# Two unused tiles that shift the start of gates, x and weight slots in SBUF

## The chip, the cores and the metric

One core of one Trainium2 chip runs the whole program. The metric is device time in microseconds (us) for one execution, from inputs in HBM to the output in HBM; lower is better. The engines named below are PE (TensorE: matmuls, with its weight loads shown as PEld), DVE (VectorE), ACT (ScalarE), POOL (GpSimd) and SP, whose queue (SPq) issues every DMA.

## The reference

Three layers in a row, with float32 results (the weights arrive as 8-byte floats):

```python
# 1. attention over chunks of 32 positions: q, k, v are (4, 8, 768, 64)
scores = scale * q_c @ k_full.T          # k_full: 8 memory rows + 16 left + 32 + 8 right
a = softmax(scores); out = a @ v_full
# x: (3072, 512), heads side by side
# 2. first gated layer, 512 -> 1536 -> 512
y = (sigmoid(x @ w_gate) * (x @ w_val)) @ w_out
# 3. second gated layer, 512 -> 2048 -> 512
h = y @ w2_in
result = (h * sigmoid(1.702 * h)) @ w2_out
```

## The kernel before, in words

**Tiling.** The 3,072 rows are cut into six blocks of 512 (`BLK`). Attention runs in 32 tiles of 96 rows, six of them ahead of the first block (the prologue), the rest beside the first gated layer. Blocks of x are kept transposed, 128 partitions by four groups (`NK`) of 512 columns. Each gated layer loops over blocks and, inside, over `f`, slices of 128 of the hidden width (`F1` = 12, then `F2` = 16).

**Split numbers.** Every operand of the large matmuls is held as a high part and a low part in a 32-bit format (F32R): `xh` and `xl`, `gh` and `gl` (the gates), and for each weight a slot of 128 x 2 x 512, high in the first 2,048 bytes of a partition and low in the next. A product is three matmuls: high by high, high by low, low by high.

**The matmuls.** All large matmuls have a stationary block of 128 x 128 (512 bytes in each partition) and stream a moving operand of 128 x 512 (2,048 bytes in each partition). `first_product` (lines 719 to 738) has the weight slot as stationary and x as moving: eight matmuls at L726, over four groups of `xh` and `xl` in turn, and four at L733 with the low weights. `gemm2` (L890, matmuls at L897) has `w_out` as stationary and `gh` or `gl` as moving, 12 a slice. `gemm4` (L993) calls `mm3` (L704): there the gate is stationary and the weight slot is moving, 12 a slice. `gated` (L742) makes the gates: a sigmoid (L750), a product (L753), the high copy (L756) and the low rest (L760). It takes the two buffers `sig0/sig1`, `gh0/gh1`, `gl0/gl1` in turn, so consecutive values of `f` use different ones.

**SBUF.** Each pool lays its tiles one behind the other, in the order in which they are opened. The long-lived pool `cp` holds, in this order, the raw and staging tiles, `sig`, `gh`, `gl`, the x tiles, one set of attention buffers (`main`, L771) and the first `NW - NLATE` of the 36 weight slots, ten of them (L779). Behind it the pool `pro` holds the prologue's attention buffers for six tiles. When the prologue has been issued, `open_late` (L810) closes `pro` and opens the other slots over the same bytes, and among them, in places that four slots take later, two raw tiles (`raw_s`), the buffers `qkn_a` and `pw_a` and an identity matrix `ident_a` for the next attention tiles. The framework makes the first use of such bytes wait for the last use of what lay there.

**Order.** `Schedule` (L32) simulates all tasks with assumed costs and due times and issues them in the resulting order; each engine then runs its own instructions in that order. Tile addresses don't enter its costs. The gate of a slot's first write (`gate`, L847 to L863) goes by the number `u` of the conversion, not by the pool in which the slot lies: from `u` = 8 (`NXR`) on, the task is ordered behind `open_late`. The weights are converted by `convert` (L231) in that order.

Of the kernel before, what the change touches and what calls it, by code (L numbers as in the profile page):

```python
# [8 lines left out]
F32 = mybir.dt.float32  # L9
# [9 lines left out]
P = 128  # L19
# [112 lines left out]
def kernel(  # L132
# [42 lines left out]
    cp = ctx.enter_context(tc.tile_pool(name="cp", bufs=1))  # L175
# [7 lines left out]
    def ring(n, shape, dtype, tag):  # L183
        return [cp.tile(shape, dtype, tag=f"{tag}{i}", name=f"{tag}{i}") for i in range(n)]
# [3 lines left out]
    NSR = 30  # L188
    raw = ring(NRAW, [P, 512], I64, "raw")
    fts = ring(NF + NST, [P, 512], F32, "f")  # L190
    sigs = ring(2, [P, BLK], F32, "sig")
    ghs = ring(2, [P, BLK], F32R, "gh")
    gls = ring(2, [P, BLK], F32R, "gl")
# [10 lines left out]


    NW = 3 * F1
    NLATE = 26
    slots = {}

    def new_slots(pool, names):  # L210
        for s in names:
            slots[s] = pool.tile([P, 2, 512], F32R, tag=f"w{s}", name=f"w{s}")
# [557 lines left out]

    main = Bufs(cp, "", ["vn", "qt", "kt", "e", "mx", "sm", "pt"])  # L771
    main.gate = None
    order = []
    for f in range(F1):
        order.append((3 * f, f, cols(w_gate, f)))
# [2 lines left out]
    order.sort(key=lambda u: u[0])  # L778
    new_slots(cp, [u[1] for u in order[: NW - NLATE]])  # L779

# [25 lines left out]
    def spare(i, shape, dtype, name):  # L806

        return late_pool[0].tile(shape, dtype, tag=f"w{order[NW - 1 - i][1]}", name=name)

    def open_late():  # L810
        pro_stack.close()
        late_pool.append(ctx.enter_context(tc.tile_pool(name="cp2", bufs=1)))
        new_slots(late_pool[0], [u[1] for u in order[NW - NLATE : NW - 4]])
        sraw.extend(spare(i, [P, 512], I64, f"raw_s{i}") for i in (3, 2))
# [268 lines left out]
```

## Time and profile before

| | |
|---|---|
| median of two timed runs | 1259.62 us (1259.45 and 1259.78) |
| profiled execution, device time | 1264.35 us |
| its span, first to last instruction | 1262.6 us |
| granted PE clock, mean of the span | 0.989 of full speed |
| PE busy | 1231.8 us (98%) |
| DVE, ACT, POOL busy | 620.2, 475.0, 236.0 us |

A busy time counts an engine as busy while any instruction is in it; neighbouring matmuls overlap in the record, so the rate of matmuls is read from the distance between their starts or from the length of a run of them, not from the length of one. The profiled execution lies 1.75 us outside its span and 4.7 us above the median; differences are worked out inside the profiled execution and then set against the median.

### The profile page before, as it was taken

Reading aid. Unit: us, or ns where it says so; the run is one execution under the profiler, and the core shown is the slowest. Engines: PE = TensorE matmul, PEld = TensorE weight load, DVE = VectorE, ACT = ScalarE, POOL = GpSimd, SP = SyncE. Lnnn points to the kernel's source line nnn. Section 1 sums busy time; section 2 is a strip of 40 time slices with the busy share of each in tenths; the row PEclk is TensorE's granted clock in tenths of the full one; section 3 lists DMA queues with packets and bytes.
Section 4 is the critical chain, followed back from the end, with each engine's and each line's share of the span. In section 5 each row is a group of like instructions: output and inputs, shape, how many; then the busy total and the mean of one; then the engine's idle time right before and its main releaser. Section 6 shows DMA issues by size and latency. Waiting matters only on the chain.

```text
span 1262.6 us, 18066 instructions
## 1 busy us (share of the span) xinstructions
PE 1231.8 (98%) x7120; PEld 987.7 (78%) x7120; DVE 620.2 (49%) x1161; ACT 475.0 (38%) x754; POOL 236.0 (19%) x198
## 2 busy tenths in 40 slices
PE   7799899999999999999999999999999999999998
PEld 5677777777777887787788788888888888888886
DVE  6979852786488528816677711122322222222322
ACT  4687742342244224313576632222222222322212
POOL 2465740010000001000365642110010000100000
PEclk9699999999999999999999999999999999999999
DMA  9556522223022202400365410010100200100000
GB/s 205 147 164 179 136 57 67 41 49 69 18 52 49 63 10 49 94 2 18 118 186 157 132 67 1 17 50 1 50 17 1 67 1 1 67 1 1 34 1 34
DMA packets 166036, 78.03 MB, mean 62 GB/s; under 512 B 132542, under 2 KB 153278, under 8 KB 165950
## 3 DMA queue, kind: packets, MB, share of 16 engines
q1 hardware_dynamic: 165950, 76.87, 23.5%
q8 instruction: 56, 0.92, 0.3%
q14 instruction: 30, 0.25, 0.1%
HBM read 64.24 MB, written 12.58 MB: 61 GB/s over the span
## 4 chain that ended last, share of the span: by engine, by line
PE 90%; DVE 5%; DMA 1%; ACT 1%; issue 1%; POOL 1%; SPq 1%; DVEq 0%; POOLq 0%; ACTq 0%
PE bank L726 33%; PE bank L704 21%; PE bank L733 17%; PE bank L897 14%; PE bank L645 2%; PE bank L495 1%; DVE f L276 1%; DVE pw L563 1%; SPq L305 1%; POOL pw_a L563 1%; PE bank L585 0%; DVE raw_s L262 0%; DVE raw L271 0%; DVE raw L262 0%; DVE sm L552 0%
## 5 line engine op out<-in xcount | busy, mean ns | idle before, releaser
L726 PE MATMUL bank<-xh,w 128*128 128x512 f32 x960 | 382.4, 398 | 2.3 <-ACT w L281 2.0
L726 PE MATMUL bank<-xl,w 128*128 128x512 f32 x960 | 380.9, 397 | 0.0
L753 DVE TENSOR_TENSOR sig<-bank,sig 128x512 f32<-128x512 f32 x168 | 115.9, 690 | 434.1 <-ACT sig L750 337.3
L733 PE MATMUL bank<-xh,w 128*128 128x512 f32 x960 | 264.1, 398 | 0.0
L750 ACT ACTIVATE sig<-bank 128x512 f32<-128x512 f32 x168 | 100.6, 599 | 389.6 <-PE bank L733 389.3
L704 PE MATMUL bank<-w,gh 128*128 128x512 f32 x768 | 241.0, 395 | 0.0
L726 PEld LDWEIGHTS bank<-xh,w 128*128 128x128 f32 x960 | 181.5, 189 | 47.9 <-ACT w L281 2.3
L726 PEld LDWEIGHTS bank<-xl,w 128*128 128x128 f32 x960 | 181.5, 189 | 43.3
L733 PEld LDWEIGHTS bank<-xh,w 128*128 128x128 f32 x960 | 179.3, 188 | 42.8
L756 ACT ACTIVATE gh<-sig 128x512 fp32r<-128x512 f32 x168 | 106.2, 632 | 197.4 <-DVE sig L753 190.3
L704 PEld LDWEIGHTS bank<-w,gh 128*128 128x128 f32 x768 | 144.6, 188 | 33.7
L897 PE MATMUL bank<-gh,w 128*128 128x512 f32 x576 | 159.6, 399 | 0.0
L704 PE MATMUL bank<-w,gl 128*128 128x512 f32 x384 | 151.1, 393 | 0.0
L897 PEld LDWEIGHTS bank<-gh,w 128*128 128x128 f32 x576 | 108.5, 190 | 26.5 <-DVE f L918 0.2
L760 DVE TENSOR_TENSOR gl<-sig,gh 128x512 fp32r<-128x512 f32 x128 | 91.0, 711 | 74.5 <-ACT gh L756 74.2
L285 POOL TENSOR_TENSOR w<-f,w 128x512 fp32r<-128x512 f32 x68 | 96.2, 1428 | 62.7 <-ACT w L281 61.1
L563 POOL TENSOR_TENSOR raw<-e,sm 96x448 f32<-96x448 f32 x21 | 21.6, 1029 | 410.8 <-DVE sm L555 410.8
L704 PEld LDWEIGHTS bank<-w,gl 128*128 128x128 f32 x384 | 72.2, 188 | 17.1
L946 POOL TENSOR_TENSOR xl<-f,xh 128x512 fp32r<-128x512 f32 x24 | 31.4, 1318 | 279.9 <-ACT xh L943 279.9
L897 PE MATMUL bank<-gl,w 128*128 128x512 f32 x288 | 79.7, 398 | 0.0
L620 DVE STREAM_TRANSPOSE pt<-raw 32x256 f32<-32x256 f32 x168 | 73.1, 435 | 2.6
L760 POOL TENSOR_TENSOR gl<-sig,gh 128x512 fp32r<-128x512 f32 x40 | 55.7, 1391 | 73.3 <-ACT gh L756 68.7
(84 smaller groups left out, 908.6 us busy)
## 6 DMA issues: line engine op xcount, KB each, us to landing
raw<-in_moe_w_out_dram SPq DMA_DIRECT2D x24, 512.0 KB
raw<-in_moe_w_in_dram SPq DMA_DIRECT2D x16, 512.0 KB
y_dram<-f SPq DMA_DIRECT2D x24, 256.0 KB
f<-y_dram SPq DMA_DIRECT2D x24, 256.0 KB
out_dram<-f SPq DMA_DIRECT2D x23, 256.0 KB
vn<-in_v_dram SPq DMA_DIRECT2D x24, 240.0 KB
raw<-in_moe_w_gate_dram SPq DMA_DIRECT2D x8, 512.0 KB
raw<-in_moe_w_val_dram SPq DMA_DIRECT2D x8, 512.0 KB
```

Of the source, the lines that this page charges most:

```text
L285: nc.gpsimd.tensor_tensor(out=w[:, 1, :], in0=ft, in1=w[:, 0, :].bitcast(F32), op=ALU.subtract)
L563: eng.tensor_tensor(out=dst, in0=e3()[r, :, c], in1=T["sm"][r].to_broadcast([n, H, keys[1] - keys[0]]), op=ALU.mult)
L620: nc.vector.transpose(T["pt"][r * CH : (r + 1) * CH, :, c * CH : (c + 1) * CH], T["pn"][c * CH : (c + 1) * CH, :, kb * CH : (kb + 1) * CH],)
L704: nc.tensor.matmul(ps_out, a, c, start=(first and i == 0 and j == 0), stop=(last and i == n - 1 and j == 2),)
L726: nc.tensor.matmul(bank[bk][:, :n], w[:, 0, ts[t]], x[xb][:, t, :n], start=t == 0 and x is xhs, stop=False)
L733: nc.tensor.matmul(bank[bk][:, :n], w[:, 1, ts[t]], xhs[xb][:, t, :n], start=False, stop=t == NK - 1)
L750: nc.scalar.activation(sig[:, :n], bank[src_sig][:, :n], AF.Sigmoid, scale=scale)
L753: nc.vector.tensor_tensor(out=sig[:, :n], in0=bank[src_val][:, :n], in1=sig[:, :n], op=ALU.mult)
L756: nc.scalar.activation(gh[:, :n], sig[:, :n], AF.Copy)
L760: eng.tensor_tensor(out=gl[:, :n], in0=sig[:, :n], in1=gh[:, :n].bitcast(F32), op=ALU.subtract)
L897: nc.tensor.matmul(bank[Y[m]][:, :n], w[:, wi, m * P : (m + 1) * P], g[:, :n], start=f == 0 and j == 0, stop=f == F1 - 1 and j == 2,)
L946: nc.gpsimd.tensor_tensor(out=xls[xb][:, m, :], in0=st[:, :BLK], in1=xhs[xb][:, m, :].bitcast(F32), op=ALU.subtract)
```

## The change

Two tiles that nothing writes or reads are opened in `cp`: `pad0`, 224 x 4 = 896 bytes a partition, ahead of `sig0`, and `pad1`, 112 x 4 = 448 bytes, behind `main` and ahead of the weight slots. `NLATE` goes from 26 to 27, so that nine slots lie in `cp` and the tenth is opened by `open_late`, as the first of the late ones. With that, `sig`, `gh`, `gl`, `xh`, `xl` and all slots begin at multiples of 2,048 bytes.

```diff
@@ -188,6 +188,7 @@
     raw = ring(NRAW, [P, 512], I64, "raw")
     fts = ring(NF + NST, [P, 512], F32, "f")
+    cp.tile([P, 224], F32, tag="pad0", name="pad0")
     sigs = ring(2, [P, BLK], F32, "sig")
     ghs = ring(2, [P, BLK], F32R, "gh")
@@ -204,7 +205,7 @@
     NW = 3 * F1
-    NLATE = 26
+    NLATE = 27
     slots = {}
@@ -770,6 +771,7 @@
     main = Bufs(cp, "", ["vn", "qt", "kt", "e", "mx", "sm", "pt"])
     main.gate = None
+    cp.tile([P, 112], F32, tag="pad1", name="pad1")
     order = []
```

## Rows read from the trace of the kernel before

**Rows 1.** Page, part 1: busy us, share of the span, instructions by engine.

```profile
PE 1231.8 (98%) x7120; PEld 987.7 (78%) x7120; DVE 620.2 (49%) x1161; ACT 475.0 (38%) x754; POOL 236.0 (19%) x198
```

**Rows 2.** Busy time by stretches: stretch, length, then each engine's busy us, granted clock.

```profile
core 0: us, PE busy (x) PEld busy (x) DVE busy (x) ACT busy (x) POOL busy (x), PEclk, DMA share, GB/s
...
49.17:54.88 5.71, 5.71 (x14) 4.45 (x14) 5.68 (x6) 3.59 (x6) 4.21 (x3) 0.50 1.13 285
...
75.00:200.00 125.00, 117.23 (x765) 92.67 (x766) 88.74 (x131) 81.97 (x131) 69.17 (x60) 0.97 0.50 131
200.00:734.00 534.00, 533.84 (x3481) 425.99 (x3480) 338.16 (x732) 215.19 (x323) 93.16 (x71) 1.00 0.28 69
734.00:1253.00 519.00, 519.00 (x2234) 419.39 (x2233) 128.32 (x182) 130.25 (x215) 43.65 (x34) 1.00 0.06 21
```

**Rows 3.** Chain that ended last, 725 to 742 us: start us, us, what, how many.

```profile
728.57 3.73 PE bank L726 x16
...
734.18 2.79 PE bank L704 x12
736.97 1.87 PE bank L726 x8
738.84 2.76 PE bank L704 x12
```

**Rows 4.** The same stretches by line: two rows L726, two L733, then L704, L897.

```profile
200.00:734.00 534.00, 238.09 (x945) 177.17 (x944) 1.00 0.28 69
734.00:1262.60 528.60, 186.66 (x736) 138.02 (x736) 1.00 0.07 23
...
200.00:734.00 534.00, 130.10 (x476) 88.53 (x476) 1.00 0.28 69
734.00:1262.60 528.60, 100.92 (x369) 69.04 (x368) 1.00 0.07 23
...
734.00:1262.60 528.60, 282.37 (x1152) 216.61 (x1151) 1.00 0.07 23
...
200.00:734.00 534.00, 195.66 (x716) 133.48 (x715) 1.00 0.28 69
```

**Rows 5.** Who waited, PE from 200 us on: us in total, times, longest.

```profile
PE bank L726 <- ACT sig L750: 0.2, 1, 0.2
```

**Rows 6.** PE in order of time, 736 to 739 us: start us, us, instruction.

```profile
736.81 0.39 PE L726 MATMUL bank<-xh,w 128*128 128x512 f32 x1
...
737.28 0.40 PE L726 MATMUL bank<-xh,w 128*128 128x512 f32 x1
...
737.74 0.40 PE L726 MATMUL bank<-xh,w 128*128 128x512 f32 x1
...
738.21 0.40 PE L726 MATMUL bank<-xh,w 128*128 128x512 f32 x1
...
738.67 0.63 PE L704 MATMUL bank<-w,gh 128*128 128x512 f32 x2
```

**Rows 7.** The same view, 740 to 742 us.

```profile
740.07 0.62 PE L704 MATMUL bank<-w,gh 128*128 128x512 f32 x2
...
741.44 0.86 PE L733 MATMUL bank<-xh,w 128*128 128x512 f32 x3
```

**Rows 8.** The same view, first and last of twelve matmuls at half clock.

```profile
49.76 0.63 PE L726 MATMUL bank<-xl,w 128*128 128x512 f32 x1
...
54.45 0.59 PE L726 MATMUL bank<-xh,w 128*128 128x512 f32 x1
```

**Rows 9.** Chain, 86 us: transposes, each with a weight load of its own.

```profile
86.37 0.44 PE bank L386 x4
```

**Rows 10.** All engines in order of time, 44 to 50 us.

```profile
44.30 2.83 PE L645 MATMUL bank<-pt,vn 128*64 128x96 f32 x32
...
47.29 0.35 SPq L305 DMA_DIRECT2D qkn_a<-in_k_dram  x1
47.34 0.21 POOL masks.py:197 MEMSET ident_a<- 128x128 f32 x1 [5.10 <-PE bank L645]
...
49.17 0.51 SPq L253 DMA_DIRECT2D raw_s<-in_moe_w_gate_dram  x1
```

## The prediction

> **What bounds the kernel now.** I read the engines' busy times first: PE is busy for 98% of the span and no other engine for half of it [rows 1]. Then the stretches: from 200 us to 1,253 us PE has no gap to speak of, at a granted clock of 1.00, while DVE falls to 128 us of the last 519 [rows 2]. The view of waits says the same: from 200 us on PE waited 0.2 us for other engines [rows 5]. Before 200 us PE is not the only bound: 117.2 of 125 us busy between 75 and 200, with the clock not always at full [rows 2]. So after 200 us the time is the number of matmuls times the distance between their starts, and nothing else that the change touches counts there. The number: 945 + 736 at L726, 476 + 369 at L733, 1,152 at L704 and 716 at L897 make 4,394 of the large kind [rows 4]. The distance, from the chain that ended last: 16 matmuls in 3.73 us, or 233.1 ns; 12 of L704 in 2.79 us, or 232.5 ns; the next 12 of L704 in 2.76 us, or 230.0 ns [rows 3]. At 233.1 ns the 4,394 take 1,024 us of the 1,062 us that follow 200 us.
>
> **What the distance is made of.** This decides the case. Twelve matmuls ran at a granted clock of 0.50 (the level of 1.2 GHz) [rows 2]. Their first and last start lie 54.45 - 49.76 = 4.69 us apart, 11 distances of 426.4 ns [rows 8]. That is 512 columns at 1.2 GHz with nothing on top. Half of it, 213.2 ns, would be the distance at 2.4 GHz if streaming were all. Measured are 233.1, so 19.9 ns, 8.5%, come on top at the upper level alone. It isn't the weight load: four transposes with a weight load of 128 columns each take 0.44 us, 110 ns for each pair [rows 9], so a load can be hidden in far less than 213 ns. What is left is that the moving operand doesn't arrive at full rate, or a fixed cost of changing from one operand to the next. The first could hang on addresses, the second would not.
>
> **The change part by part.** *The pads.* They add no instruction and move no work. Before, `sig`, the gates and x began 2,048 - 896 = 1,152 bytes past a multiple of 2,048, and the slots, shifted by both pads (1,344 bytes), 704 past one. Every moving operand is 2,048 bytes long, so today each crosses one multiple of 2,048, and after the change none does. Of the four stationary blocks of 512 bytes in a half of a slot, one crosses today (704 + 2 x 512 = 1,728 to 2,240), after the change none.
>
> *Stationary side.* Here the trace has the comparison. At L726 each block serves two matmuls; the four pairs start at 736.81, 737.28, 737.74 and 738.21 and end with the next start at 738.67: 0.47, 0.46, 0.47 and 0.46 us [rows 6]. The third pair has the crossing block and takes what the others take. I cost this at nothing; the bound is the reading error, 0.01 us a pair.
>
> *Moving side.* No large matmul in this trace streams an operand that doesn't cross, so the cost is bounded by rows. From below: the same crossing operands cost nothing at half clock [rows 8]. From above: a crossing can cost no more than the whole excess of 19.9 ns. Between them lies the one sign that addresses matter at all: the groups of L704 alternate between 2.79 and 2.76 us [rows 3]. They do the same work; what alternates with `f` is the pair of gate buffers and the slot. The two run at the same offset inside 2,048 bytes in both groups, so this 2.5 ns comes from higher address bits, which the change moves but doesn't sort. I take nothing for the alignment itself, as the value nearest to rows 6 and 8, and keep 0 to 19.9 ns. Below nothing can't be excluded: all streams and weight loads will start at the same offset, which they don't today. What else hangs on those high bits: the faster groups of L704, 48 x 12 = 576 matmuls, may lose their 2.5 ns (+1.4 us), or the other 576 may gain it (-1.4 us).
>
> *The tenth slot and the shift of the late ones.* Slot number 9 moves to `open_late`, and late tiles lie over other attention buffers than before. Its conversion was ordered behind `open_late` already (`u` from 8 on), so the order of instructions stays. New waits can arise on ACT (the high copy into that slot), on SP (`raw_s` now lies over the last tile's `pw` and `vn`, not its `qn`, `kn`, `pw`) and on POOL. All of it waits at most for the last prologue tile, whose product at L645 ends at 44.30 + 2.83 = 47.13; `qkn_a` on SP and `ident_a` on POOL wait for it today (47.29, 47.34), and the first `raw_s` load is issued at 49.17, behind them in SP's queue [rows 10]. That is a cover of 2.0 us, so the cost is 0. Queued behind a late `raw_s` load would be the next loads on SP, and DVE's conversions wait for those; without the cover the price is at most the 2.83 us of L645. `ident_a` will lie behind all old buffers and can be made earlier, but POOL's next instruction (`pw_a`) still waits, so nothing is gained.
>
> *Other engines.* DVE, ACT and POOL read and write the shifted tiles too. After 200 us they are covered by PE; before, a few ns on each of some hundred instructions stay under 1 us.
>
> *The sum.* 0 for the stationary blocks, 0 for the moving operand with 0 to -87 us (4,394 x 19.9 ns) kept as its bound, -1.4 to +1.4 for the alternating groups, 0 to +2.8 for the late slots. The profiled execution would stay at 1264.35 us. The median lies 4.7 us below it; the same difference leaves 1259 us.
>
> **The rivals.** B, *a partial gain*: aligned streams run as in the faster groups. For: such a distance exists in this trace at all. Price: (233.1 - 230.0) ns x 3,818 (without the 576) = 11.8 us, so 1248 us; at the best six distances of such a group, 740.07 to 741.44 [rows 7], 228.3 ns, 19 us, so 1240 us. Against: L726 streams x at four places and never leaves 0.46 to 0.47 us a pair [rows 6].
>
> C, *the excess is the crossing*: it goes, and the distance falls to 213.2 ns: 3,818 x 19.9 + 576 x 16.8 = 86 us, so 1174 us. For: the excess has the same size wherever the moving operand crosses. Against: one crossing in the middle of a stream has to cost as much as 48 columns; the place of the crossing differs (896 bytes in for x, 1,344 for the slots) with 233.1 against 232.5 ns; and rows 8 show none of it. The Trainium skill, "TensorE: Matmul & The Clock Gate", section "Back-to-back issue gap", gives N / 2.4 + 2.5 ns for matmuls back to back, 215.8 ns here. By that rule 17.3 ns of each distance would be avoidable; an estimate from that page is a saving of some 74 us, 1185 us. The trace doesn't agree with that rule as it stands (233.1 ns), and no run here yet shows why.
>
> D, *slower*: weight load and stream now begin at the same offset within 2,048 bytes, and if both are served by one part of SBUF they collide in every matmul. It decides from 25.2 / 4,394 = 5.7 ns a matmul, 2% of 1259.62 us. At the size that rows 3 show for an address effect, 3.1 ns the other way, it is +13.6 us, 1273 us; with the excess doubled, 1347 us. For: rows 3 show that addresses can matter. Against: at L726 no pair differs, whichever block of the slot is loaded meanwhile. The Trainium skill, "SBUF — State Buffer", section "Who interferes with whom", says that PE waits for no other user of SBUF, with one read port for the stream and one for the weights; by that rule D can't happen. The 2.5 ns between the groups of rows 3 are something that this rule doesn't explain.
>
> E, *the late slots wait after all*: the cover of 2.0 us is too short, and the prologue ends up to 2.8 us later: 1262 us.
>
> **How the numbers follow.** A, the forecast: 46%, 1257 to 1262 us. B: 22%. C: 13%. D: 14%. E: 5%. The time is A's, 1259 us. About 2% is what a measurement of this kernel can tell from no change: faster is below 1234.4 us, slower above 1284.8 us. C and the far end of B (a distance below 227.4 ns, 5%) make 18% faster; D beyond 5.7 ns is 6% slower; 76% lie between. The range takes A, B, E and the nearer part of D: 1230 to 1276 us; it leaves out C and the far part of D, some 19%.
>
> **What would show it.** Right: sixteen matmuls of L726 in the chain again in 3.73 us, the pairs again 0.46 to 0.47 us, half-clock matmuls at 426 ns, and SP's first `raw_s` load within 0.5 us of 49.2. B shows as both kinds of L704 groups, and L726, at 2.76 us or less for twelve; C as 3.45 us or less for sixteen; D as more than 3.8 us for sixteen. E shows as an SP wait on L645 behind `qkn_a`. The prediction is wrong if the moving operand's start sets its rate, which no row of before could show since every stream crosses.

## The result and the profile after

The changed kernel takes 1238.83 us (two runs, 1238.0 and 1239.65) against 1259.62 us, a ratio of 0.983 with a 95% interval of 0.981 to 0.985: 1.7% faster. The profiled execution takes 1238.0 us, its span is 1236.2 us; that is 26.4 us less than the span before. The kernel issues the same 18,066 instructions. In its line numbers L726, L733, L704 and L897 have become L727, L734, L705 and L899.

Page, part 1, of the changed kernel, which answers to [rows 1]:

```profile
PE 1201.4 (97%) x7120; PEld 983.8 (80%) x7120; DVE 625.0 (51%) x1161; ACT 474.4 (38%) x754; POOL 232.5 (19%) x198
```

PE is still the bound, with 30 us less of it. The chain that ended last, in the stretch that answers to [rows 3] (start us, us, what, how many):

```profile
715.51 3.63 PE bank L727 x16
...
720.95 2.72 PE bank L705 x12
...
725.48 2.72 PE bank L705 x12
```

Sixteen matmuls of the first product now take 3.63 us, 226.9 ns each, where [rows 3] had 3.73. Twelve of `gemm4` take 2.72 us, 226.7 ns, in both alternating groups, where [rows 3] had 2.79 and 2.76. So the large matmuls became faster by 3 to 6 ns, and all have the same distance now. At half clock nothing changed (PE in order of time, the counterpart of [rows 8]):

```profile
48.10 0.63 PE L727 MATMUL bank<-xl,w 128*128 128x512 f32 x1
...
50.24 0.63 PE L727 MATMUL bank<-xh,w 128*128 128x512 f32 x1
```

Five distances take 50.24 - 48.10 = 2.14 us, 428 ns, against 426.4 before; the granted clock is 0.50 there too, and the difference is within the reading error (0.01 us on each start). The gain shows at the upper clock level alone.

**Where the 26.4 us are.** Of the 4,394 matmuls after 200 us, 3,242 went from 233.1 to 226.9 ns (20.1 us) and 1,152 from 231.3, the mean of the two groups, to 226.7 ns (5.3 us); together 25.4 us. The same work begins some 2 us earlier now, so its waits are read from 195 us on, where the kernel before has the same 0.2 us as in [rows 5]. PE now waits a little more for others:

```profile
PE bank L727 <- ACT sig L751: 1.3, 2, 1.1
PE bank L899 <- DVE f L920: 0.6, 1, 0.6
PE bank L727 <- DVE sig L754: 0.2, 1, 0.2
```

That is 2.1 us against 0.2, so 1.9 us are given back. The first large matmul started at 47.51 instead of 49.17, 1.7 us earlier. This sums to 25.2 of 26.4 us. Whether the prologue's 1.7 us are owed to the change is not shown: two kernels below that differ only in a pad of 192 or 128 bytes start at 47.90 and 49.35 us, but the four kernels with the larger pads (this one among them) start at 46.7 to 47.6 and the four others at 47.9 to 49.4.

### The profile page after: what moved, and what is told of

The parts are those of the page before. It is cut to its first block, busy times and chain, and to the rows that moved or that the text cites. A ratio compares the mean times of both kernels' runs of the same rounds, so it can differ in the third digit from the quotient of the medians.

```text
span 1236.2 us, 18066 instructions
## 1 busy us (share of the span) xinstructions
PE 1201.4 (97%) x7120; PEld 983.8 (80%) x7120; DVE 625.0 (51%) x1161; ACT 474.4 (38%) x754; POOL 232.5 (19%) x198
## 4 chain that ended last, share of the span: by engine, by line
PE 79%; DVE 10%; DMA 4%; SPq 2%; issue 2%; POOL 2%; ACT 1%; DVEq 0%; POOLq 0%; ACTq 0%
PE bank L727 29%; PE bank L705 21%; PE bank L734 14%; PE bank L899 11%; DMA raw<-in_moe_w_out_dram 2%; DVE f L277 2%; SPq L306 2%; PE bank L646 2%; DVE raw L272 2%; PE bank L496 1%; DVE raw L263 1%; DVE raw_s L263 1%; DVE pw L564 1%; DMA raw<-in_moe_w_in_dram 1%; POOL w L286 1%
## 5 line engine op out<-in xcount | busy, mean ns | idle before, releaser
L727 PE MATMUL bank<-xh,w 128*128 128x512 f32 x960 | 376.8, 393 | 4.4 <-ACT sig L751 2.0
L727 PE MATMUL bank<-xl,w 128*128 128x512 f32 x960 | 375.2, 391 | 0.0
L734 PE MATMUL bank<-xh,w 128*128 128x512 f32 x960 | 257.4, 392 | 0.0
L705 PE MATMUL bank<-w,gh 128*128 128x512 f32 x768 | 236.4, 389 | 0.0
L727 PEld LDWEIGHTS bank<-xh,w 128*128 128x128 f32 x960 | 181.4, 189 | 45.2 <-ACT sig L751 3.7
L727 PEld LDWEIGHTS bank<-xl,w 128*128 128x128 f32 x960 | 181.4, 189 | 37.7
L734 PEld LDWEIGHTS bank<-xh,w 128*128 128x128 f32 x960 | 178.7, 188 | 37.5
L705 PEld LDWEIGHTS bank<-w,gh 128*128 128x128 f32 x768 | 144.2, 188 | 29.8
L899 PE MATMUL bank<-gh,w 128*128 128x512 f32 x576 | 156.1, 393 | 0.6 <-DVE f L920 0.6
L705 PE MATMUL bank<-w,gl 128*128 128x512 f32 x384 | 149.4, 389 | 0.0
L899 PEld LDWEIGHTS bank<-gh,w 128*128 128x128 f32 x576 | 108.0, 189 | 24.1 <-DVE f L920 1.1
L705 PEld LDWEIGHTS bank<-w,gl 128*128 128x128 f32 x384 | 72.1, 188 | 15.0
L899 PE MATMUL bank<-gl,w 128*128 128x512 f32 x288 | 78.1, 393 | 0.0
```

The lines of the kernel that those rows point to most:

```text
L705: nc.tensor.matmul(ps_out, a, c, start=(first and i == 0 and j == 0), stop=(last and i == n - 1 and j == 2),)
L727: nc.tensor.matmul(bank[bk][:, :n], w[:, 0, ts[t]], x[xb][:, t, :n], start=t == 0 and x is xhs, stop=False)
L734: nc.tensor.matmul(bank[bk][:, :n], w[:, 1, ts[t]], xhs[xb][:, t, :n], start=False, stop=t == NK - 1)
L899: nc.tensor.matmul(bank[Y[m]][:, :n], w[:, wi, m * P : (m + 1) * P], g[:, :n], start=f == 0 and j == 0, stop=f == F1 - 1 and j == 2,)
```

## The experiments

Below, *phase* is the start of the stream (moving operand) minus the start of the stationary block, modulo 256 bytes. Stationary blocks lie 512 bytes apart and groups of x 2,048, so all matmuls of one kind have one phase. Whether the block in use counts or the one that is loaded meanwhile, no run separates. Before the change it was (1,152 - 704) modulo 256 = 192 in the first products and `gemm2`, and (704 - 1,152) modulo 256 = 64 in `gemm4`; after the change it is 0 everywhere. The theories on trial in the first four runs: M, a stream that crosses a multiple of some unit pays; S, the stationary block does; P, the two starts must agree.

**Only gates and x aligned.** The second pad is left out of the changed kernel:

```diff
-    cp.tile([P, 112], F32, tag="pad1", name="pad1")
```

> Only the first pad: gates and x begin at multiples of 2,048 bytes, the slots 1,600 bytes past one. Theory M (a stream that crosses a multiple of 2,048 pays, the stationary side doesn't count): sixteen matmuls of the first products and of gemm2 at 3.63 us as in the changed kernel, twelve of gemm4, whose stream is the slot, stay at 2.76 to 2.79 us; 1,152 matmuls x 4 to 6 ns are lost against the changed kernel, so 1244 us, ratio 0.988. Theory S (it is the stationary block): gates are aligned as stationary, so gemm4 alone gains, 1254 us. Theory P (stream and load must begin at the same offset): nothing gains, 1259 us.

Measured: 1261.28 us, ratio 1.000 (0.999 to 1.001). The chain of this kernel:

```profile
726.09 3.73 PE bank L727 x16
...
731.69 2.76 PE bank L705 x12
...
736.31 2.76 PE bank L705 x12
```

The streams of the first product begin on a multiple of 2,048 and cross none, and still take 3.73 us for sixteen. Alignment of the stream alone gains nothing here, against M with the unit 2,048. S falls too, for `gemm4`, whose stationary gates are aligned, takes 2.76 in both groups, where S needs 2.72 ([rows 3] have 2.79 and 2.76). Phases here: 192 in the first product, 64 in `gemm4`, as before.

**Only the slots aligned.** The first pad is left out, the second is 336 x 4 bytes:

```diff
-    cp.tile([P, 224], F32, tag="pad0", name="pad0")
-    cp.tile([P, 112], F32, tag="pad1", name="pad1")
+    cp.tile([P, 336], F32, tag="pad1", name="pad1")
```

> Only the slots begin at multiples of 2,048 bytes; gates and x stay 1,152 past one. Theory M: gemm4 goes to 2.72 us for twelve, all others stay at 3.73 us for sixteen; 1,152 x 4 to 6 ns, so 1254 us, ratio 0.995. Theory S: first products and gemm2, whose stationary block is the slot, go to 3.63 us for sixteen and gemm4 stays, 1244 us. Theory P: nothing gains, 1259 us.

Measured: 1261.74 us, ratio 1.000 (0.999 to 1.001).

```profile
723.43 3.73 PE bank L726 x16
...
729.01 2.80 PE bank L704 x12
```

`gemm4`, now with an aligned stream, takes 2.80 us, no less than before. The phase is 128 everywhere. Neither half of the change gains anything alone.

**All 1,024 bytes off.** The first pad grows, so that gates, x and slots all begin 1,024 bytes past a multiple of 2,048:

```diff
-    cp.tile([P, 224], F32, tag="pad0", name="pad0")
+    cp.tile([P, 480], F32, tag="pad0", name="pad0")
```

> Gates, x and slots all begin 1,024 bytes past a multiple of 2,048, so each stream crosses one multiple of 2,048 in its middle and stream and load keep the same offset. Theory M with the unit 2,048: 3.73 us for sixteen, 1259 us. Theory M with a unit of 1,024 or less, and theory P: 3.63 us for sixteen, 1239 us.

Measured: 1236.76 us, ratio 0.980 (0.979 to 0.982), the full gain, with every stream crossing a multiple of 2,048:

```profile
719.93 2.72 PE bank L705 x12
722.65 1.81 PE bank L727 x8
```

That leaves P, or an alignment of both sides to a unit of 1,024 bytes or less.

**Lone streams.** Runs of 24 matmuls on one filled tile, in lines of their own:

> Leaves out the reference's work: 41 runs of 24 matmuls on one filled tile, one run a line, each with its own start of the moving operand or of the stationary block or its own number of columns; the output is not the reference's. Theory M: the run length hangs on the moving start alone, about 5.4 us for 24 where no multiple of the unit is crossed and 0.15 us more where one is; with the unit 2,048 only starts of 0 and 2,048 are short, with 1,024 also 1,024, with 512 also 512 and 1,536. Stationary starts change nothing. Theory S: moving starts change nothing and stationary starts do. Theory P: the runs with the same offset on both sides (+704, +1,024, +1,152) are short. A fixed cost for each operand: the 256-column runs have the same excess over half of 213.2 ns as the 512-column ones.

The chain of this kernel; each row is one line with 24 matmuls:

```profile
30.18 5.44 PE bank L45 x24
35.62 5.51 PE bank L46 x24
41.13 5.58 PE bank L47 x24
46.71 5.46 PE bank L48 x24
...
63.22 5.60 PE bank L51 x24
...
79.88 5.46 PE bank L54 x24
...
123.84 5.60 PE bank L62 x24
...
135.02 5.44 PE bank L64 x24
...
157.03 5.49 PE bank L68 x24
...
168.01 5.45 PE bank L70 x24
173.46 2.88 PE bank L71 x24
...
179.22 2.74 PE bank L73 x24
...
193.37 4.18 PE bank L78 x24
...
205.88 4.16 PE bank L81 x24
210.03 5.49 PE bank L82 x24
```

L45 to L56 move the stream's start, with the block at a multiple of 512: by 0, 64, 128, 256, 704, 1,024 and 1,152 bytes. 0, 256 and 1,024 are short (5.44 to 5.46 us, 227 ns each, crossing or not), 64 takes 5.51, 128 and 1,152 take 5.58, 704 (192 modulo 256) takes 5.60, 233.3 ns each. All nine multiples of 256 that were run, up to 2,048, take 5.44 to 5.46, and no other start of the stream in this run does. So the unit is 256. L62 to L65 move the block instead, by 64, 256 and 448 bytes: 5.60, 5.44 and 5.49, the values of phases 192, 0 and 64. L70 moves both by 1,152 bytes and takes 5.45, as at phase 0. L68 and L69 move both by 704 and by 1,024 bytes and take 5.49, 2 ns a matmul more than the other lines at phase 0. The chain in two windows of L68 shows where:

```profile
157.03 2.32 PE bank L68 x10
...
159.35 3.17 PE bank L68 x14
```

The first ten take 232 ns each and the last fourteen 226 ns, the value of phase 0; the line ahead of it is at phase 128. So the distances need some matmuls to settle behind a run of another phase, and what is carried over is open. Once settled, the difference of the starts decides. Theory P holds for 512 columns, with 256 bytes for its unit; S and M, each with one side alone, fall here for good.

The effect belongs to the length of the stream. L71 and L73 are streams of 256 columns at phases 0 and 192: 2.88 and 2.74 us, so there phase 0 is the worse one. L78 and L81 are streams of 384 columns at phases 0 and 192: 4.18 and 4.16 us, no phase to speak of. The mark of a fixed cost was that 256 columns have the same excess as 512. At phase 0 they do: 120.0 - 106.6 = 13.4 ns, and 13.5 with 512 columns. At phase 192 they don't (7.6 and 20.1 ns). So a fixed cost could be the part that phase 0 leaves, but not the phase. L82 to L85 are considered below.

**The same phase without alignment.** The kernel before, with one pad of 192 bytes ahead of the slots:

```diff
     main.gate = None
+    cp.tile([P, 48], F32, tag="pad1", name="pad1")
```

> The kernel before with one pad of 192 bytes ahead of the slots and nothing else; NLATE stays 26. Gates and x stay 1,152 bytes past a multiple of 2,048, slots are 896 past: neither lies on a multiple of 512 and every stream crosses a multiple of 2,048, but stream and load begin 256 bytes apart modulo 512, so at the same place modulo 256. Theory P256 (what counts is the distance of the two starts modulo 256): 226.7 ns a matmul, sixteen of L726 in 3.63 us, 1237 us, ratio 0.980. Theory M1024 (both sides must lie on multiples of 1,024, or of 512): 3.73 us and 1260 us as before.

Measured: 1237.93 us, ratio 0.982 (0.980 to 0.983).

```profile
715.67 3.63 PE bank L726 x16
...
721.11 2.72 PE bank L704 x12
```

The whole gain, with no operand on a multiple of 512 and ten slots opened at first. This decides between P and the alignment of both sides to 256 bytes or more in the kernel itself. Both sides lie on multiples of 128 here, but so they do with only the slots aligned, which gained nothing.

**Phase 64 instead of 192.** The same line with a pad of 128 bytes (`[P, 32]`):

> The kernel before with a pad of 128 bytes ahead of the slots: x and gates minus slots is 64 modulo 256 where they are the stream, and 192 in gemm4. Theory P256, with the lone streams' values: first products and gemm2 at 229 ns (sixteen in 3.66 us), gemm4 at 233.3 ns (twelve in 2.80 us); 3,242 x 4.4 - 1,152 x 1.5 ns, so about 1248 us, ratio 0.990. Theory M: nothing changes, 1260 us.

Measured: 1253.81 us, ratio 0.994 (0.992 to 0.996).

```profile
721.40 3.66 PE bank L726 x16
...
726.89 2.80 PE bank L704 x12
729.70 1.86 PE bank L726 x8
```

The order of the phases is as expected: sixteen of L726 at 3.66 us, twelve of `gemm4`, now at 192, at 2.80. The size is 7 us instead of 12 by the medians, 9.1 by the spans of the profiled executions (1262.6 and 1253.5 us). A part is seen: eight matmuls of L726 that follow a group of `gemm4` take 1.86 us, as at phase 192, and not 1.83, which fits the carrying over seen in L68. The rest was not followed up.

**The tenth slot alone.** The kernel before with `NLATE = 27`:

> NLATE = 27 alone, no pads. Every theory: no effect, 1260 us, ratio within 0.998 to 1.002; if the moved slot or the shifted late tiles cost or gain anything before 200 us, it shows here alone.

Measured: 1260.93 us against 1260.85, ratio 1.000 (0.999 to 1.001). The moved slot costs nothing. Its chain:

```profile
733.08 2.76 PE bank L704 x12
...
737.71 2.79 PE bank L704 x12
```

By the layout, gates, x and slots lie where they did before: the tenth slot, now the first of the late ones, takes the same bytes. Yet the groups of `gemm4` alternate the other way round than in [rows 3], 2.76 first and then 2.79.

**What the stream collides with.** More lone streams:

> Leaves out the reference's work: 34 runs of 24 matmuls on one filled tile, each run with its own distance between the starts of stream and load (0 to 240 bytes in steps of 16), number of loaded columns, or width of the numbers. Theory P256, collisions of the weight load with the stream: 5.44 us for 24 at phase 0, more at 64 to 192; a load of 64 or 32 columns has fewer collisions and comes nearer to 213.2 ns (5.3 us for 24); numbers of 16 bits leave room between reads and show no phase. A fixed cost for each stream: 226.7 ns stays at phase 0 with loads of 32 columns and with 16-bit numbers too. If the phase counts only while the load lasts, halves at 0 and 192 run like phase 0, halves at 192 and 0 like phase 192.

The chain of this kernel, 24 matmuls a row:

```profile
29.29 5.44 PE bank L62 x24
...
96.08 5.59 PE bank L74 x24
101.67 5.63 PE bank L75 x24
...
118.34 5.52 PE bank L78 x24
123.86 5.49 PE bank L79 x24
...
140.44 5.55 PE bank L82 x24
145.99 5.56 PE bank L83 x24
...
173.65 5.52 PE bank L88 x24
179.16 5.60 PE bank L89 x24
...
189.96 5.18 PE bank L91 x24
...
205.50 5.20 PE bank L94 x24
210.70 5.19 PE bank L95 x24
```

L62, L74, L75 and L77 are phases 0, 192, 208 and 240: 5.44, 5.59, 5.63 and 5.45. Of the sixteen phases only 0 and 240 reach 5.45, and 208 is the slowest. L78 and L79 load 96 columns at phases 0 and 192 (5.52, 5.49, the order turned round), L80 and L81 load 64 (5.52, 5.57), L82 and L83 load 32 (5.55, 5.56). So the phase matters less with a shorter load and hardly at all with the shortest, which would fit a meeting of load and stream; but a short load does not come nearer to 213.2 ns, against the expectation: 5.55 us is 231 ns. That load and stream meet is therefore argued, not shown. Loading the same block each time changes nothing (L84, L85). With the first half of a stream at phase 0 and the second at 192 (L88) it takes 5.52, the other way round (L89) 5.60: the first half decides most of it, the second a part. Dense 16-bit numbers take 5.18 us, 216 ns, at phases 64 and 192 (L91, L93), so they show no phase, as expected. Streams of 480 columns show none either (L94, L95): 5.20 and 5.19 us at phases 0 and 192. Their 216.7 ns lie 16.8 above their share of 213.2, so one fixed cost for all lengths doesn't fit.

**Width or span.** The last run:

> Leaves out the reference's work. First, 16-bit numbers taken from every second place, so that a stream covers the same 2,048 bytes as a 32-bit one: if the excess comes from the bytes that a stream spans, 24 take 5.4 to 5.6 us with the phase seen again; if it comes from the width of the numbers, 5.18 us as with dense 16-bit numbers, at every phase. Then groups of twelve as gemm4 issues them, at the addresses of the kernel before, each behind eight first-product matmuls: if the alternation of 2.79 and 2.76 us is one of the addresses of gates and slots, even groups take 2.79 and odd ones 2.76; if it hangs on the order in which the kernel comes to them, all are alike. Phase 0: 2.72 us.

Its chain; L68 and L71 have 24 matmuls, the others are groups of 12:

```profile
30.14 5.44 PE bank L68 x24
...
46.41 5.44 PE bank L71 x24
...
75.40 2.76 PE bank L77 x12
...
80.03 2.79 PE bank L79 x12
...
84.69 2.76 PE bank L81 x12
...
89.33 2.79 PE bank L83 x12
```

16-bit numbers from every second place take 5.44 us at phases 0 and 192 (L68, L71), not 5.18: the excess doesn't go with the width of the numbers. It goes with the span of bytes that a stream covers, or with the step between its numbers; no run separates these two. The phase has all but gone there, which P256 doesn't explain. L77 and L79 are the even and the odd groups of `gemm4` at their old addresses: 2.76 and 2.79, the alternation of [rows 3], but the other way round. L81 (odd gates with the even slot) and L83 (even gates with the odd slot) show that it doesn't go with the gates. Even and odd slots come in turn here, though, so a dependence on the slot can't be told from one on the order. As lone streams all four take 5.49 us (L82 to L85 of the earlier run), and with `NLATE` alone the alternation was turned round at the same addresses. So the slot's address alone doesn't make it. That each group takes something over from the one ahead of it, as L68 of the lone streams does, fits all of these rows; what is taken over is open.

## Why the prediction was right and wrong

The time moved by less than 2% and lies inside 1230 to 1276 us, as forecast. The forecast time was wrong: 1259 us was case A, no change, and what came is case B, a partial gain, 1 us beyond its far end of 1240. That the range holds it is owed to B being let into it, not to the mechanism that was forecast.

*What bounds the kernel* held. The time after 200 us is the number of matmuls times their distance, and 25.4 of the 26.4 us are that product.

*The moving side* is the step that failed: "I take nothing for the alignment itself". It measured 6.2 ns for each of 3,242 matmuls and 4.6 ns for each of 1,152, inside the bounds of 0 to 19.9 ns that I had kept. I took the nearest rows to be 6 and 8, and neither could show the effect. In [rows 6] all four pairs have one and the same phase, for blocks lie 512 bytes apart; the comparison varied the crossing, which doesn't count, and held fixed what does. [Rows 8] are at half clock, where the excess is gone in both kernels. The nearest to a sign of it was the 2.76 of [rows 3], `gemm4` at phase 64, but the 2.79 beside it has the same phase.

*What the distance is made of* ruled the weight load out by its length, 110 ns for a pair in [rows 9]. That a load fits in doesn't make it free: where its block starts moved the distance by up to 6.7 ns here (L62 against L64).

*That this 2.5 ns comes from higher address bits* was argued, and is not shown. The two groups have the same phase, the lone streams don't tell them apart, and `NLATE` alone turned the alternation round at the same addresses. What makes it is open.

*The stationary side* at nothing was right for crossings and wrong as a whole: the block's start counts as much as the stream's, since it is their difference that decides.

*Rival B* had the right mark, rows at 230.0 ns, and was mis-sized: its best distance was 228.3 ns, and 226.7 came. Its sign, 2.76 us or less for twelve in both kinds of groups, is there (2.72). *Rival C*, the excess as the price of a crossing, fell: 13.5 of the 19.9 ns stay, and a stream that crosses is as fast as one that doesn't (L54, and the run with all at 1,024). The formula N / 2.4 + 2.5 ns of the Trainium skill, "TensorE: Matmul & The Clock Gate", section "Back-to-back issue gap", which calls it the gap of an isolated matmul, makes 215.8 ns at 512 columns. Dense 16-bit streams measure just that here (216 ns, L91); 32-bit streams of 512 columns stay above it at every phase.

*Rival D* had load and stream meet, with the sign reversed: I argued that equal starts would collide, and equal starts are the best case for streams of 512 columns. Its decision point, 5.7 ns above the kernel before, wasn't reached in any run: the slowest of sixteen phases, 208, takes 5.63 us for 24, 1.5 ns a matmul above 233.1. The Trainium skill, "SBUF — State Buffer", section "Who interferes with whom", gives PE one read port for the stream and one for the load, and calls them independent. These runs don't bear out that independence: the start of the block alone changes the distance of the matmuls by up to 6.7 ns (L62 against L64).

*The late slots* at nothing was right. `raw_s` is again issued 1.88 us behind `qkn_a` (45.63 and 47.51; [rows 10] have 47.29 and 49.17); that it doesn't come within 0.5 us of 49.2 goes with the whole prologue, which ends earlier. `NLATE` alone gives 1.000:

```profile
45.63 0.35 SPq L306 DMA_DIRECT2D qkn_a<-in_k_dram  x1
...
47.51 0.51 SPq L254 DMA_DIRECT2D raw_s<-in_moe_w_gate_dram  x1
```

*The sum.* With 6.2 and 4.6 ns in place of 0, the same sum gives -25.4 us, 1234 us against the median. The median of the changed kernel lies 4.6 us above that. The two timed runs of the kernel before lie low in what its other runs take (1258.6 to 1264.8 us in 19 runs, median 1261.77): beside those, the runs at phase 0 gain 25.0 us (1261.77 to 1236.76) and 22.9 us (1260.85 to 1237.93).

## What to carry to other kernels

Where PE streams 32-bit operands back to back, compare the distance of matmul starts with half of the distance at the lower clock level; here the excess over it went away at half clock, and 6 of its 20 ns hung on where the operands lie. With streams of 512 columns and loads of 128, look at the difference of the starts of stream and stationary block, modulo 256 bytes, before aligning anything: one pad of 192 bytes did here what two pads and a moved slot did. Other lengths have to be measured, for 256 columns turn the order round and 384 and 480 show no effect. When a row is taken as evidence that addresses don't matter, ask which part of the address it varies.

## What the runs showed of the hardware that was not expected

- The distance of 128 x 512 matmuls with 32-bit operands and loads of 128 columns depends on the starts of stream and stationary block by their difference modulo 256 bytes: 226.7 ns at 0, 229 to 230 at 64, 232.5 at 128, 233.3 at 192. 512 columns at the upper clock level alone would be 213.2, half of the 426.4 ns of [rows 8].
- The order of phases belongs to the length of the stream: with 256 columns, phase 192 is shorter (2.74 us for 24) than phase 0 (2.88); with 384 and 480 columns the two are alike (4.16 and 4.18, 5.19 and 5.20).
- Distances settle: behind a run of another phase, the first ten matmuls of a run at phase 0 took 232 ns each and the next fourteen 226 (L68 of the lone streams).
- 16-bit numbers taken from every second place stream no faster than 32-bit ones (5.44 us for 24), dense ones do (5.18).
- What remains at phase 0, 13.5 ns a matmul, doesn't shrink with a shorter load (5.55 us for 24 with 32 columns loaded, 5.44 with 128), and is 13.4 ns with 256 columns but 16.8 with 480. Its cause stays open.
